# A recurrent attention and two feed-forward layers: decay products stored head first, and feed-forward units that follow the weight blocks as they are made

## The chip, the cores and the metric

The kernel runs on one core of a Trainium2 chip. The metric is the device time of one execution in microseconds (us). Three executions of the kernel before took 1311.25, 1311.51 and 1312.43 us; the median is 1311.51 us. One more execution was profiled.

## The reference

Three parts follow each other. The first is a recurrence over 768 time steps for 4 batches x 8 heads = 32 heads of width 40, each with a 40 x 40 state. The other two are gated feed-forward layers over 3072 rows of 320 values.

```python
for t in range(S):
    y[:, :, t] = np.einsum('bhd,bhde->bhe', rt, state)
    Sa = np.einsum('bhde,bhe->bhd', state, at)
    state_decay = state * wt[:, :, None, :] - np.einsum('bhd,bhe->bhde', Sa, bt)
    state = state_decay + np.einsum('bhd,bhe->bhde', vt, kt)
...
g = x @ w_gate                            # 320 x 1536
silu = g * (1.0 / (1.0 + np.exp(-g)))     # layer 1; layer 2 has only the sigmoid here
x = (silu * (x @ w_val)) @ w_out          # 1536 x 320
```

## The kernel before

**The recurrence by chunks.** Time is cut into 12 chunks of 64 steps (`C = 64`). Inside a chunk everything is matrix products; between chunks only the state is carried. The keys, `a` and the results of a chunk are scaled by running products of the decay `w` along the chunk (powers `p`) and by their inverses (`r`). For chunks 0 to 3 these products come from scans on VectorE. For chunks 4 to 11 GpSimd multiplies them up ahead of time, four chunks at once, with one head and chunk on each partition (`powers`, lines 228 to 269), and SyncE stores them to DRAM: `pd[m]` and `rd[m]`, at line 268. There are two such groups, so 8 stores of `p` and 8 of `r`. Both groups use the same two tiles (`wp`, `wq`), so the second group may write them only when the stores of the first have landed. The loads of a later chunk read them back with time on the partitions: `load_p` (`pn`, line 350, read twice for each chunk), `loads` (`ip`, line 338) and `ends` (line 372).

**What a chunk consists of.** `prep_a(m)` scales and builds `kps` products, `prep_b(m)` inverts a triangular matrix (on VectorE, with two trips through DRAM for chunks from 3 on: `xd`, lines 534 and 536), `chain(m)` carries the state and `post(m)` makes the output rows. `merge` (line 913) interleaves the generators of these parts by a table of steps and offsets (`NA`, `NB`, ... lines 924 to 939): while `chain` and `post` of chunk m run, `prep_b` of m + 1 and `prep_a` of m + 2 are emitted beside them, and `ahead(m)`, which is the first feed-forward layer on the output of chunk m - 1. A scheduler then sets the order on each engine; every engine carries out its own instructions in that order.

**The feed-forward layers by units.** The 3072 rows are 12 blocks of 256 rows, one for each chunk. The 1536 columns are 12 weight blocks. A unit is one block of rows with one weight block: `gate` makes 16 matrix products of 128x256 (line 1105) and the gating (lines 1109 to 1112), `add` sums 6 products of 128x320 into two accumulators (line 1121). Every weight arrives as 64-bit floats and is split into a high and a low part by `load_w`, in three thirds; the last step of the last third is line 1031 on GpSimd. A layer has 12 x 12 = 144 units, the two together 288.

**Which units run when.** During the recurrence memory has room for few weight blocks of layer 1 (`w1`): three early, two more during chunk 1, and seven that `more` (line 1312) puts into tiles that the recurrence gives up near its end. `extra(m)` runs block m with the blocks that exist when it starts: `used.append(len(w1))` (line 1332). After the recurrence `stream` runs what is left of layer 1 for each row block (`w1[used[blk]:]`, adding to the part already in DRAM), while the weights of layer 2 are converted (`ahead`, line 1361), and then layer 2.

**Names in the rows.** `tp` transposes, `kps`, `zps`, `xps`, `qps`, `ups`, `sps`, `aps`, `yps` are matrix products of the recurrence, `am` is the masked `aps`, `gv` is the gate product during the recurrence and `g` after it, `hh` and `hl` are the high and low part of a unit's gated values, `po` the accumulators. `part_...` are several small tiles of the recurrence that share memory; the tile `an`, which line 386 writes, and the one that line 534 reads are both such pieces of one `part`. `raw` is a third of a weight block as it arrives, `dt` and `ds` its work tiles.

## Time and profile before

| | before |
|---|---|
| median of three executions | 1311.51 us |
| the profiled execution, its own time | 1313.94 us |
| span of its instructions | 1312.2 us |
| PE busy in the span | 1212.9 us (92%) |
| DVE, ACT, POOL busy | 714.0, 600.9, 562.0 us |

PE is TensorE's matrix products, PEld its weight loads, DVE VectorE, ACT ScalarE, POOL GpSimd, SP SyncE, which here only issues DMAs. PEclk is the TensorE clock that was granted, 1.0 being full. Between stretches of the program the limits differ: the recurrence with the units beside it ends about 677 us into the span; what follows are feed-forward units alone. In a row of an engine's timeline the square bracket is the idle time of the engine before the instruction, and what ended it.

### The profile page before, as it was taken

The page shows a single profiled execution, that of the slowest core. Times are in us where ns is not written, and L with a number is a line of the kernel's source. Part 1 is how long each engine was busy: PE and PEld are TensorE (multiplying, and loading weights), DVE is VectorE, ACT ScalarE, POOL GpSimd, SP SyncE. Part 2 cuts the span into 40 slices and gives each one's busy share as a digit, 9 for nine tenths or more (in the row PEclk, how much of TensorE's full clock was granted, in tenths as well). Part 3 has the DMA queues.
Part 4 walks back from the last instruction along what each step waited for, and adds up shares of the span by engine and source line. Part 5 has one row for each costly group of instructions (what it writes and reads, how often), then busy time and mean ns, then how long its engine had stood idle before and what let it go on. Part 6 is the DMA issues. An engine that isn't in the chain of part 4 may idle for free.

```text
span 1312.2 us, 34352 instructions
## 1 busy us (share of the span) xinstructions
PE 1212.9 (92%) x14209; PEld 1164.6 (89%) x14209; DVE 714.0 (54%) x1434; ACT 600.9 (46%) x1447; POOL 562.0 (43%) x749
## 2 busy tenths in 40 slices
PE   5487889999999999898899999999999999999996
PEld 4477778989988998797889999999999999999996
DVE  6858668886668867757789877222111212212121
ACT  8464655655665566254434444223333333333331
POOL 5757352232233233457778988322222222222221
PEclk7666977999999999799899999999999999999998
DMA  7554844433454344343455542221000000000000
GB/s 214 118 135 120 201 120 123 127 105 113 131 150 126 89 117 108 104 108 112 169 175 171 185 159 94 95 97 45 11 23 23 23 23 23 23 23 23 11 11 14
DMA packets 153061, 126.12 MB, mean 96 GB/s; under 512 B 100928, under 2 KB 131136, under 8 KB 152640
## 3 DMA queue, kind: packets, MB, share of 16 engines
q1 hardware_dynamic: 152896, 123.84, 32.7%
q8 instruction: 113, 1.85, 0.6%
q14 instruction: 52, 0.43, 0.1%
HBM read 92.05 MB, written 31.76 MB: 94 GB/s over the span
## 4 chain that ended last, share of the span: by engine, by line
PE 58%; DVE 20%; ACT 8%; DMA 4%; issue 4%; POOL 3%; SPq 1%; ACTq 0%; POOLq 0%; DVEq 0%
PE g L1105 31%; PE po L1121 16%; DVE pr L521 4%; PE gv L1105 3%; DVE part L527 3%; PE kps L481 2%; DMA wt<-in_a_w_dram 2%; PE tp L366 1%; PE aps L854 1%; DVE dt L1008 1%; DVE am L863 1%; ACT bn L490 1%; DVE lq L493 1%; ACT bn L491 1%; DVE g L1110 1%
## 5 line engine op out<-in xcount | busy, mean ns | idle before, releaser
L1105 PE MATMUL g<-x,w 128*128 128x256 f32 x3520 | 485.9, 282 | 2.1 <-DVE g L1110 1.3
L1105 PEld LDWEIGHTS g<-x,w 128*128 128x128 f32 x3520 | 456.7, 189 | 3.2 <-DVE g L1110 2.1
L1112 POOL TENSOR_TENSOR hl<-g,hh 128x256 fp32r<-128x256 f32 x288 | 225.8, 785 | 474.1 <-ACT hh L1111 466.3
L1110 DVE TENSOR_TENSOR g<-g,g 128x256 f32<-128x256 f32 x220 | 92.9, 423 | 361.8 <-PE g L1105 353.3
L1121 PE MATMUL po<-w,hh 128*128 128x320 f32 x1152 | 228.9, 312 | 4.8 <-ACT hh L1111 4.7
L1111 ACT CAST hh<-g 128x256 fp32r<-128x256 f32 x288 | 116.7, 406 | 252.9 <-DVE g L1110 222.8
L1121 PEld LDWEIGHTS po<-w,hh 128*128 128x128 f32 x1152 | 177.1, 189 | 6.6 <-ACT hh L1111 6.1
L1105 PE MATMUL gv<-x,w 128*128 128x256 f32 x1088 | 160.7, 298 | 7.9 <-DVE g L1110 6.0
L1105 PEld LDWEIGHTS gv<-x,w 128*128 128x128 f32 x1088 | 143.4, 199 | 12.9 <-DVE g L1110 9.2
L1121 PE MATMUL po<-w,hl 128*128 128x320 f32 x576 | 143.7, 314 | 2.5 <-POOL hl L1112 2.5
L1109 ACT ACTIVATE g<-g 128x256 f32<-128x256 f32 x220 | 84.3, 384 | 130.4 <-PE g L1105 123.9
L1025 POOL TENSOR_TENSOR dt<-dt,w 128x384 f32<-128x384 f32 (+1 forms) x72 | 80.4, 1118 | 82.3 <-DVE ds L1012 36.8
L1121 PEld LDWEIGHTS po<-w,hl 128*128 128x128 f32 x576 | 93.7, 190 | 3.8 <-POOL hl L1112 3.5
L493 DVE TENSOR_TENSOR lq<-kps,part 64x256 f32<-64x256 f32 x96 | 40.5, 421 | 84.2 <-ACT bn L491 66.4
L521 DVE TENSOR_TENSOR pr<-part,sn 128x4 f32<-128x4 f32 (+4 forms) x135 | 74.7, 553 | 3.6
L481 PE MATMUL kps<-lq,kbt 104*128 104x128 f32 x384 | 62.6, 314 | 8.4 <-DVE lq L493 6.9
L527 DVE TENSOR_REDUCE part<-pr 128x2 f32<-128x4 f32 (+4 forms) x135 | 66.5, 493 | 2.8
L1023 ACT CAST w<-dt 128x384 fp32r<-128x384 f32 (+1 forms) x72 | 35.5, 495 | 66.9 <-DVE dt L1008 62.2
L481 PEld LDWEIGHTS kps<-lq,kbt 104*128 104x128 f32 x384 | 54.8, 220 | 12.4 <-issue 4.2
L854 PE MATMUL aps<-rbd,ut 104*128 104x128 f32 x384 | 56.3, 292 | 5.5 <-DVE am L863 5.1
L1007 DVE TENSOR_SCALAR dt<-dt 128x384 int32<-128x384 int32 (+1 forms) x72 | 44.9, 624 | 30.0 <-POOL dt L1004 29.6
L490 ACT ACTIVATE bn<-kps 32x256 f32<-32x256 f32 x96 | 35.8, 373 | 50.0 <-PE kps L481 43.9
(182 smaller groups left out, 1670.9 us busy)
## 6 DMA issues: line engine op xcount, KB each, us to landing
raw<-in_w_dram SPq DMA_DIRECT2D x48, 384.0 KB
xd<-x SPq DMA_DIRECT2D x12, 896.0 KB
x<-xd SPq DMA_DIRECT2D x12, 896.0 KB
raw<-in_w_dram SPq DMA_DIRECT2D x24, 320.0 KB
ld<-in_a_kb_dram SPq DMA_DIRECT2D x22, 320.0 KB
ld<-rd SPq DMA_DIRECT2D x32, 160.0 KB
pn<-pd SPq DMA_DIRECT2D x32, 160.0 KB
ld<-in_a_a_dram SPq DMA_DIRECT2D x12, 320.0 KB
```

What stands on the lines that cost most here:

```text
L481: nc.tensor.matmul(kps[:, n].rearrange("p h t -> p (h t)"), lhsT=kbt[0:PW, n, :], rhs=lq[m % 3][0:PW, 4 * g4 + n].rearrange("p h t -> p (h ...
L493: nc.vector.tensor_tensor(out=lq[m % 3][o, q, h2, :], in0=kps[o, :, h2, :], in1=mask[o, None, :].to_broadcast([64, 4, C]), op=ALU.mult,)
L521: nc.vector.tensor_tensor(out=o, in0=xs[:, 0:kk, None, 0:n].to_broadcast([P, kk, 2, n]), in1=sn[:, None, n : n + 2, 0:n].to_broadcast([P, ...
L527: nc.vector.tensor_reduce(out=xs[:, 0:kk, n : n + 2], in_=o, axis=AX.X, op=ALU.add)
L854: nc.tensor.matmul(aps[:, n, h2], lhsT=ut[0:PW, x, 2 * h2 : 2 * h2 + 2].rearrange("p u s -> p (u s)"), rhs=rbd[0:PW, x, h2].rearrange("p b ...
L1025: sub(out=tf, in0=tf, in1=w.bitcast(F32), op=ALU.subtract)
L1105: nc.tensor.matmul(gv[n], lhsT=p, rhs=q, start=e == 0, stop=e == len(seq) - 1)
L1109: nc.scalar.activation(out=g, in_=gv[0], func=AF.Silu if silu else AF.Sigmoid)
L1110: nc.vector.tensor_tensor(out=g, in0=gv[1], in1=g, op=ALU.mult)
L1111: nc.scalar.copy(out=hh, in_=g)
L1112: self.heng.tensor_tensor(out=hl, in0=g, in1=hh.bitcast(F32), op=ALU.subtract)
L1121: self.nc.tensor.matmul(ops[u], lhsT=p[:, us], rhs=q, start=first and n == 0, stop=last and n == 2)
```

## The change

**Storage.** `pd[m]` and `rd[m]` are laid out head first, `[heads, time, 40]`, as the tiles are, so a store takes 65 x 40 or 64 x 40 values of one head in one run (10,400 or 10,240 bytes) instead of 160 bytes at a time. The loads of chunks 4 to 11 gather: `pn` takes 16 heads x 64 steps in pieces of 40 values (160 bytes; before 2,560), `ip` 8 heads x 64 steps (160 bytes; before 1,280) in two DMAs where there was one.

**Units.** `ffn` asks for the next weight block after each unit, so a block that was appended to `w1` meanwhile is used too; the number used is noted at the end. The numbers by row block change from 3, 5 (eight times), 6, 8, 11, in all 68, to 3, 5 (eight times), 7, 10, 12, in all 72. Row block 11 is then finished, and the stream after the recurrence has 11 jobs of layer 1, with 72 units instead of 76. The two tiles for a block's rows alternate by place in that list.

```diff
--- before.py
+++ after.py
@@ -264,8 +264,8 @@
             rows = slice(32 * j, 32 * j + 32)
             for i, x in enumerate((p[rows], q[rows, 1:])):
                 to = (pd, rd)[i]
-                to[m] = dr.tile([C + 1 - i, H * B, D], F32, tag=f"{'pr'[i]}d{m}", name="pr"[i] + "d", bufs=1)
-                nc.sync.dma_start(out=to[m].rearrange("t h d -> h t d"), in_=x)
+                to[m] = dr.tile([H * B, C + 1 - i, D], F32, tag=f"{'pr'[i]}d{m}", name="pr"[i] + "d", bufs=1)
+                nc.sync.dma_start(out=to[m], in_=x)
             yield
 
     def all_powers():
@@ -335,10 +335,11 @@
             dma(out=x, in_=kb[m, bp])
 
             for u in range(2):
-                dma(
-                    out=ip[HALF[u]].rearrange("t (c x) -> t c x", c=2),
-                    in_=rd[m].rearrange("t (c u x) d -> t c u (x d)", c=2, u=2)[:, :, bp],
-                )
+                for c in range(2):
+                    dma(
+                        out=ip[HALF[u]].rearrange("t (c x d) -> t c x d", c=2, d=D)[:, c],
+                        in_=rd[m].rearrange("(c u x) t d -> t c u x d", c=2, u=2)[:, c, bp],
+                    )
             yield x, ip
 
     def load_p(m):
@@ -347,7 +348,10 @@
             nc.sync.dma_start(out=pn, in_=pq[m])
             return pn
         for b2 in range(2):
-            nc.sync.dma_start(out=pn[HALF[b2]], in_=pd[m][0:C, 16 * b2 : 16 * b2 + 16].rearrange("t h d -> t (h d)"))
+            nc.sync.dma_start(
+                out=pn[HALF[b2]].rearrange("t (h d) -> t h d", d=D),
+                in_=pd[m][16 * b2 : 16 * b2 + 16, 0:C].rearrange("h t d -> t h d"),
+            )
         return pn
 
     def loads_late(m):
@@ -369,7 +373,7 @@
         return ps
 
     def ends(m):
-        nc.sync.dma_start(out=pairs(pe[0:NS])[:, 0], in_=pd[m][C].rearrange("(s h) d -> s h d", h=2))
+        nc.sync.dma_start(out=pairs(pe[0:NS])[:, 0], in_=pd[m][:, C].rearrange("(s h) d -> s h d", h=2))
         yield
         ps = ptp.tile([P, 4, P], F32, tag="tp", name="pep")
         nc.tensor.transpose(ps[0:PW, 0, 0:NS], pe[0:NS, 0], ident[0:NS, 0:NS])
@@ -1125,14 +1129,16 @@
     def ffn(self, x, ws, silu, tag):
 
         ops, pend = self.sums(tag), None
-        for f, w in enumerate(ws):
-            h = self.gate(x, w, silu)
+        self.o, f = ops, 0
+        while f < len(ws):
+            h = self.gate(x, ws[f], silu)
             if pend is not None:
-                self.add(ops, *pend)
-            pend = w, h, f == 0, f == len(ws) - 1
-            yield
-        self.add(ops, *pend)
-        self.o = ops
+                self.add(ops, *pend, False)
+            pend = ws[f], h, f == 0
+            f += 1
+            yield
+        self.add(ops, *pend, True)
+        self.used = f
 
     def stream(self, jobs):
 
@@ -1329,11 +1335,11 @@
                 if m == 0:
                     ffn.raw = raws
                 if m >= 0:
-                    used.append(len(w1))
                     x = ffn.split(ys.pop(m))
                     nc.sync.dma_start(out=xd[m], in_=x.bitcast(F32))
                     yield
-                    yield from ffn.ffn(x, w1[: used[m]], True, "po")
+                    yield from ffn.ffn(x, w1, True, "po")
+                    used.append(ffn.used)
                     for u in range(2):
                         ob = h_p.tile([P, DM], F32, tag="ob", name="ob", bufs=1)
                         nc.scalar.copy(out=ob, in_=ffn.o[u])
@@ -1360,8 +1366,10 @@
 
             ahead = load_w2()
 
+            left = [blk for blk in range(NB) if used[blk] < NF]
+
             def load_x(blk):
-                ffn.x = (x_q, x_p)[blk % 2]
+                ffn.x = (x_q, x_p)[left.index(blk) % 2]
                 x = ffn.new_x()
                 nc.sync.dma_start(out=x.bitcast(F32), in_=xd[blk])
                 yield x
@@ -1372,7 +1380,7 @@
                 nc.sync.dma_start(out=xin[:, :, 0:DM], in_=src)
                 nc.sync.dma_start(out=xin[:, :, DM:], in_=src[:, :, 256:DM])
                 yield
-                ffn.x = (x_q, x_p)[blk % 2]
+                ffn.x = (x_q, x_p)[(len(left) + blk) % 2]
                 yield from ffn.split_steps([xin[:, 0], xin[:, 1]])
 
             parts = {}
@@ -1383,7 +1391,7 @@
                     nc.sync.dma_start(out=part, in_=xs[1][2 * blk : 2 * blk + 2].rearrange("u p e -> p u e"))
                 if 1 <= f <= 3:
                     next(ahead, None)
-                if blk == NB - 1 and f == NF - 1 - used[blk]:
+                if blk == left[-1] and f == NF - 1 - used[blk]:
                     for _ in ahead:
                         pass
 
@@ -1428,7 +1436,7 @@
                 flag.append(fl)
 
             flag, jobs, seen = [], [], []
-            for blk in range(NB):
+            for blk in left:
                 jobs.append((w1[used[blk] :], True, "po", load_x(blk), partial(each1, blk), partial(end1, blk)))
             for blk in range(NB):
                 jobs.append((w2, False, "po", split_x(blk), partial(check, blk), partial(end2, blk)))
```

The change makes the scheduler set another order in places. On POOL, just after the first group's powers, `L261` is the second group's first write to `wp`. Before:

```order
L1004 TENSOR_SCALAR dt<-dt 128x384
L238 TENSOR_TENSOR wq<-wq 128x320 x2
L1025 TENSOR_TENSOR dt<-dt,w_1450 128x384
L238 TENSOR_TENSOR wq<-wq 128x320
L1027 TENSOR_TENSOR w_1450<-dt,ds 128x256
L1029 TENSOR_TENSOR w_1450<-dt,ds 64x128
L238 TENSOR_TENSOR wq<-wq 128x320
L261 MEMSET wp 128x40
L238 TENSOR_TENSOR wq<-wq 128x320
L1004 TENSOR_SCALAR dt<-dt 128x384
L238 TENSOR_TENSOR wq<-wq 128x320 x2
```

And now:

```order
L1008 TENSOR_SCALAR dt<-dt 128x384
L238 TENSOR_TENSOR wq<-wq 128x320 x2
L261 MEMSET wp 128x40
L1029 TENSOR_TENSOR dt<-dt,w_1450 128x384
L238 TENSOR_TENSOR wq<-wq 128x320
L1031 TENSOR_TENSOR w_1450<-dt,ds 128x256
L1033 TENSOR_TENSOR w_1450<-dt,ds 64x128
L238 TENSOR_TENSOR wq<-wq 128x320 x2
L1008 TENSOR_SCALAR dt<-dt 128x384
L238 TENSOR_TENSOR wq<-wq 128x320 x2
L1029 TENSOR_TENSOR dt<-dt,w_1450 128x384
```

The write to `wp` stands five rows earlier, right behind the second of the `wq` products and before the conversion of a weight third; nothing else moves there.

On DVE, in the same part of the program, `L241` clamps the second group's decays, once for `wp` and once for `wq`; `sps` and `kps` are products of chunks 0 and 1. Before:

```order
L726 TENSOR_TENSOR part_86<-sps,part_86 40x4x2x40 x2
L1008 SCALAR_TENSOR_TENSOR dt<-raw,dt 128x384
L726 TENSOR_TENSOR part_86<-sps,part_86 40x4x2x40 x2
L727 TENSOR_TENSOR part_86<-part_86,pend 104x4x2x40
L1012 TENSOR_SCALAR ds<-dt 128x384
L241 TENSOR_SCALAR wp<-wq 128x2560
L727 TENSOR_TENSOR part_86<-part_86,pend 104x4x2x40
L493 TENSOR_TENSOR lq_210<-kps,part_86 64x4x64
L1013 SCALAR_TENSOR_TENSOR ds<-raw,ds 128x384
L863 TENSOR_TENSOR am<-aps,part_86 128x512
L241 TENSOR_SCALAR wq<-wq 128x2560
```

And now:

```order
L497 TENSOR_TENSOR lq_210<-kps,part_86 64x4x64
L241 TENSOR_SCALAR wp<-wq 128x2560
L497 TENSOR_TENSOR lq_210<-kps,part_86 64x4x64
L1011 TENSOR_SCALAR dt<-dt 128x384
L241 TENSOR_SCALAR wq<-wq 128x2560
L1012 SCALAR_TENSOR_TENSOR dt<-raw,dt 128x384
L730 TENSOR_TENSOR part_86<-sps,part_86 40x4x2x40 x2
L497 TENSOR_TENSOR lq_210<-kps,part_86 64x4x64
L730 TENSOR_TENSOR part_86<-sps,part_86 40x4x2x40 x2
L1016 TENSOR_SCALAR ds<-dt 128x384
L731 TENSOR_TENSOR part_86<-part_86,pend 104x4x2x40
```

Both clamps now stand ahead of the additions of `sps` (L730, before L726), where they stood behind them.

On SP, in one chunk of the middle stage, from the loads of `pn` on. Before:

```order
L350 DMA pn<-pd 64x640 x2
L335 DMA ld<-in_a_kb_dram 128x640
L338 DMA ld<-rd 64x2x320 x2
L1334 DMA xd<-x 128x1792
L534 DMA xd<-part_88 1024x1x32 x2
L356 DMA part_197<-in_a_v_dram 64x640 x2
L536 DMA part_212<-xd 32x16x32 x4
L335 DMA ld<-in_a_kb_dram 128x640
```

And now:

```order
L351 DMA pn<-pd 64x16x40 x2
L335 DMA ld<-in_a_kb_dram 128x640
L339 DMA ld<-rd 64x8x40 x4
L1339 DMA xd<-x 128x1792
L538 DMA xd<-part_88 1024x1x32 x2
L360 DMA part_197<-in_a_v_dram 64x640 x2
L540 DMA part_212<-xd 32x16x32 x4
L335 DMA ld<-in_a_kb_dram 128x640
```

Four gathering loads of `rd` stand in front of the stores `xd<-part` where there were two, and one more pair behind; in every second chunk only one stands in front. On PE and POOL the order inside these chunks is the same as before, but for two `po` products.

On PE, at the end of the recurrence, while the last chunk's `aps` and `yps` are made; `w_8423` before and `w_8485` now are the eighth weight block. Before:

```order
L854 MATMUL aps<-rbd,ut 128x128 x4
L1105 MATMUL gv<-x,w_8423 128x256 x8
L1051 MATMUL xtp<-ident,ysb 128x128 x3
L1121 MATMUL po_8518<-w_7801,hh 128x320 x2
L1121 MATMUL po_8519<-w_7801,hh 128x320 x2
L854 MATMUL aps<-rbd,ut 128x128 x4
L1121 MATMUL po_8518<-w_7801,hl 128x320
L1121 MATMUL po_8519<-w_7801,hl 128x320
L1121 MATMUL po_8518<-w_8423,hh 128x320 x2
L1121 MATMUL po_8519<-w_8423,hh 128x320 x2
L885 MATMUL yps<-part_197,rbd 64x40 x16
```

And now:

```order
L858 MATMUL aps<-rbd,ut 128x128 x4
L1109 MATMUL gv<-x,w_8527 128x256 x3
L1109 MATMUL gv<-x,w_8745 128x256 x2
L1125 MATMUL po_8580<-w_8485,hh 128x320 x2
L1125 MATMUL po_8581<-w_8485,hh 128x320 x2
L1109 MATMUL gv<-x,w_8745 128x256 x9
L1125 MATMUL po_8580<-w_8485,hl 128x320
L1125 MATMUL po_8581<-w_8485,hl 128x320
L1109 MATMUL gv<-x,w_8745 128x256 x5
L1055 MATMUL xtp<-ident,ysb 128x128 x3
L889 MATMUL yps<-part_197,rbd 64x40 x16
L889 MATMUL yps<-tkb_91,am 64x40 x16
```

Where only the last two units' `po` products were left to run between the last `aps` and `yps`, the products of a ninth and a tenth weight block now stand there (`w_8527`, `w_8745`).

## Rows read from the trace of the kernel before

**Rows 1.** Busy time by stretch: us, PE, PEld, DVE, ACT, POOL, PEclk, DMA share, GB/s.

```profile
54.00:97.00 43.00, 32.62 (x672) 28.91 (x672) 25.84 (x45) 23.81 (x54) 24.64 (x31) 0.62 0.65 144
212.00:503.00 291.00, 282.43 (x4652) 263.14 (x4652) 220.99 (x448) 179.22 (x436) 84.32 (x98) 1.00 0.44 119
503.00:546.00 43.00, 36.88 (x566) 34.21 (x565) 32.84 (x71) 20.66 (x49) 15.71 (x20) 0.88 0.30 85
546.00:588.00 42.00, 39.23 (x637) 37.03 (x637) 25.39 (x52) 21.42 (x49) 23.91 (x33) 0.92 0.43 120
588.00:641.00 53.00, 43.56 (x552) 40.28 (x550) 38.60 (x63) 22.95 (x57) 38.24 (x52) 0.94 0.32 101
641.00:677.00 36.00, 33.08 (x238) 31.71 (x238) 28.79 (x63) 15.54 (x41) 27.37 (x35) 0.94 0.62 202
677.00:1312.00 635.00, 621.97 (x4919) 620.24 (x4919) 215.38 (x431) 222.21 (x563) 257.37 (x354) 0.99 0.19 60
```

**Rows 2.** Page, costliest groups: count, then busy us and mean ns.

```profile
L1105 PE MATMUL g<-x,w 128*128 128x256 f32 x3520 | 485.9, 282 | 2.1 <-DVE g L1110 1.3
```

**Rows 3.** SP's queue in order of time: start us, us, what it issues.

```profile
54.51 7.90 SPq L268 DMA_DIRECT2D pd<-wp  x4
...
70.27 7.22 SPq L268 DMA_DIRECT2D rd<-wq  x4
77.60 2.63 SPq L993 DMA_DIRECT2D raw<-in_w_dram  x2
81.96 0.33 SPq L236 DMA_DIRECT2D wq<-in_a_w_dram  x1
...
136.72 7.71 SPq L268 DMA_DIRECT2D rd<-wq  x4
```

**Rows 4.** POOL in order of time, 60 to 75 us.

```profile
67.05 0.14 POOL L261 MEMSET wp<- 128x40 f32 x1 [2.52 <-DMA pd<-wp]
```

**Rows 5.** DVE in order of time, 60 to 95 us.

```profile
68.52 1.01 DVE L1007 TENSOR_SCALAR dt<-dt 128x384 int32<-128x384 int32 x1 [5.48 <-POOL dt L1004]
...
83.75 0.43 DVE L493 TENSOR_TENSOR lq<-kps,part 64x256 f32<-64x256 f32 x1 [5.52 <-ACT bn L491]
...
88.96 1.49 DVE L241 TENSOR_SCALAR wp<-wq 128x2560 f32<-128x2560 f32 x1
```

**Rows 6.** ACT in order of time, 78 to 90 us.

```profile
82.63 0.55 ACT L1001 ACTIVATE dt<-raw 128x384 f32<-128x384 f32 x1 [1.05 <-DMA raw<-in_w_dram]
```

**Rows 7.** Short stretches, SP alone: us, PEclk, DMA share, GB/s.

```profile
55.00:63.00 8.00, 0.50 1.01 171
85.00:90.00 5.00, 0.97 0.57 208
562.00:565.00 3.00, 1.00 0.59 92
```

**Rows 8.** SP's queue inside one chunk of the middle stage.

```profile
332.67 1.62 SPq L350 DMA_DIRECT2D pn<-pd  x2
...
335.59 1.30 SPq L534 DMA_DIRECT2D xd<-part  x2
```

**Rows 9.** POOL in the same chunk.

```profile
341.41 1.55 POOL L386 TENSOR_TENSOR part<-ld,pn 128x640 f32<-128x640 f32 x1 [4.24 <-DMA xd<-part]
344.32 0.74 POOL L1112 TENSOR_TENSOR hl<-g,hh 128x256 fp32r<-128x256 f32 x1 [1.36 <-ACT hh L1111]
```

**Rows 10.** PE in the same chunk.

```profile
346.26 0.31 PE L1121 MATMUL po<-w,hl 128*128 128x320 f32 x1
```

**Rows 11.** PE while the last chunk is finished, 588 to 641 us.

```profile
600.98 0.85 PE L1121 MATMUL po<-w,hh 128*128 128x320 f32 x4 [1.46 <-ACT hh L1111]
...
636.99 1.13 PE L885 MATMUL yps<-part,rbd 104*64 104x40 f32 x32 [2.90 <-DVE am L863]
```

**Rows 12.** POOL, last step of two weight blocks.

```profile
612.10 0.87 POOL L1031 TENSOR_TENSOR w<-dt,ds 128x320 fp32r<-128x320 f32 x1
...
642.93 0.86 POOL L1031 TENSOR_TENSOR w<-dt,ds 128x320 fp32r<-128x320 f32 x1
```

## The prediction

> **What bounds the kernel now.** I read busy time by stretch first. From 677 us to the end PE is busy 621.97 of 635.00 us at a granted clock of 0.99 [rows 1]: feed-forward units alone, bound by PE. From 212 to 503 us it is busy 282.43 of 291.00 us at full clock [rows 1], so that stage too is almost only PE's own work. The reader is to see that what is left lies elsewhere: before 212 us, as from 54 to 97 us, where PE is busy 32.62 of 43 us and the clock is 0.62, and between 503 and 677 us, where the recurrence runs out [rows 1]. Next come the timelines, to see who is waited for there. In the early stretch SP stands at its stores of the powers: four stores hold its queue 7.90, 7.22 and 7.71 us (three of the four groups of four) [rows 3], POOL waits 2.52 us for them to land [rows 4], DVE 5.48 us for POOL [rows 5], and ACT 1.05 us for a weight third that was issued behind them [rows 6]. While the last chunk is finished, PE waits for the units' `hh` and for `am`, 1.46 and 2.90 us [rows 11]. In the middle stage POOL waits 4.24 us for the stores `xd<-part` [rows 9], but PE hardly waits.
>
> So an edit pays here only if it shortens the early stretch or puts PE's work into the holes between 546 and 677 us; and it costs if it opens holes between 212 and 503 us.
>
> **Stores (part one of the change).** All 16 stores carry 5.28 MB. From 55 to 63 us nothing but such 160-byte pieces moved: 171 GB/s at a DMA share of 1.01. From 85 to 90 us the decays came in runs of 10,240 bytes: 208 GB/s at 0.57, that is 365 GB/s for a full share [rows 7]. A store of 0.333 MB thus goes from 1.95 to 0.91 us, and four in a row from some 7.5 us to 3.6 us. SP's freed time is not itself on the path; what stood behind it is.
>
> - POOL's early write to `wp` waits for the first four stores. They will have landed at about 54.5 + 3.6 = 58 us, before POOL gets there: 2.52 us [rows 4]. The same 2.52 us leave DVE's wait for POOL [rows 5]; that is the same gain, counted once.
> - The `rd` stores start about 2.5 us earlier and hold SP to about 71 us instead of 77.5, so the weight thirds are issued from there and ACT's wait goes: 1.05 us [rows 3, 6].
> - The second group's decays can be loaded at about 72 us instead of 81.96 [rows 3]; 1.31 MB at 365 GB/s are 3.6 us, so they are there near 77 us. The two clamps of 1.49 us [rows 5] now stand early in DVE's queue, and DVE has a hole of 5.52 us that ends at 83.75 [rows 5]. They go into it and leave the dense stretch after 88.96: 2.98 us. If the load is late, all of DVE's queue stands behind the clamp, the additions of `sps` first; that is why I don't take more than their own length.
>
> Sum 6.6 us. Against it: PE ran at half clock, 0.50 in the row from 55 to 63 us [rows 7], and was busy for most of the stretch, so part of what DVE and POOL gain waits for PE. The second pair of store groups I count at nothing, because PE has other work by then. The least is nothing, or a loss the size of one new stall like DVE's (5.5 us), since PE's and DVE's order changes in this whole stretch; the most is all of SP's freed time, 4 x (7.5 - 3.6) = 15.5 us. I take a gain of 5 us, near the named waits.
>
> **Loads (part one).** A chunk's loads of `pn` and `rd` carry 1.31 MB, in 12 DMAs instead of 8. No row has 160-byte pieces loaded. The nearest is 562 to 565 us, almost only the loads `part<-xd` in pieces of 128 bytes: 92 GB/s at a share of 0.59, or 156 GB/s [rows 7], against 365. So 8.4 us instead of at least 3.6: 4.8 us more of the DMA engines for each chunk, which takes the share from 0.44 [rows 1] to about 0.56 over some 41.6 us. That alone is hidden.
>
> What is late next is `xd<-part`, for it stands behind these loads on SP, and POOL waits for it. Half of the extra bytes lie in front, 2.4 us, and two more issues; two issues take 1.30 us where each makes 1,024 pieces and 1.62 us for the coarser `pn` [rows 8], so the count of pieces doesn't matter and I take 0.65 each, 1.3 us. `xd<-part` lands up to 3.7 us later. Behind POOL's waiting instruction stands the unit's `hl`, which had 1.36 us of idle before it and was done 1.20 us before PE took it up (344.32 + 0.74 against 346.26) [rows 9, 10]. Slack 2.56 us, so PE waits at most 1.1 us. In every second chunk only one `rd` load stands in front and the slack suffices. Eight chunks: 0 to 4.5 us. A gain is excluded, since every load only gets longer. I take a loss of 1.5 us.
>
> Here the Trainium skill (DMA: Bandwidth & Descriptors, section Specifications) speaks against the change: it wants transfers of at least 512 bytes for line rate and says that below this the engine reads, modifies and writes. The trace agrees in the rate: 156 to 169 GB/s for the small pieces against 365 [rows 7]. If the rule asks no more than that, the sum stays as it is.
>
> **Units (part two).** After 677 us 3520 products are 220 units of 16 [rows 2], so one costs 635 / 220 = 2.89 us. Four fewer there: 11.5 us off the end. The four come back earlier: one in 546 to 588 us, two in 588 to 641, one in 641 to 677. PE's idle time in these is 2.8, 9.4 and 2.9 us [rows 1]. What they fill is the gain. Near the end of the second stretch the new order puts the products of two more weight blocks exactly where PE waited 2.90 us for `am` [rows 11]; the waits near 601 us lie earlier than the added units and stay. I take 4 us filled there, 1 us in the first stretch, nothing in the last, which is units alone already. The clock in these stretches is 0.92 to 0.94 [rows 1]; 6% of 43.56 us are 2.6 us, and I give 1 us of it back for the closed hole. Gain 5 + 1 = 6 us. The ends: all 11.5 us, or nothing, and below nothing by some 2 us if the added `hl` (0.74 us each, rows 9) and its gating stand in front of the recurrence on POOL, ACT and DVE.
>
> The weight blocks are there: the tenth is done at 613 us and used near 636, the twelfth at 643.8 and used near 675 [rows 12]. Costing nothing: the job that goes (its loads and stores lie at a DMA share of 0.19 [rows 1]), the alternation of the two row tiles, the stop flag. Layer 2's weight conversion loses some 11 us of room; DVE is busy 215 of 635 us there [rows 1].
>
> **Sum.** -5 + 1.5 - 6 = -9.5 us. The profiled execution took 1313.9 us, so 1304.4 by its own measure; it was 2.4 us above the median of 1311.5, which gives 1302.0 for a median.
>
> **Rivals.**
>
> 1. The small pieces into on-chip memory cost twice what the nearest row says (78 GB/s), and the middle stage pays. Then half a chunk's loads takes 8.4 us in front of `xd<-part` instead of 1.8, which with the issues is 7.9 us later; less the slack, PE waits 5.3 us in four chunks, and about 0.8 us in the four with one `rd` load in front: 24 us. With the gains 1311.5 - 11 + 24 = 1324.5, slower. It decides from about 4 us of delay of `xd<-part` in every chunk. For it: no row shows such loads, and POOL does wait there [rows 9]. Against it: 128-byte loads and 160-byte stores ran alike [rows 7]. A second cost for a partial write, beside the rate, would be the skill's rule above at its worst; no run here shows it yet. Chance 0.12.
> 2. The added units fill nothing, because PE's holes come from the recurrence's own chain and only shift: 1311.5 - 5 + 1.5 = 1308. For it: the larger holes are waits for ACT and DVE [rows 11], which the units load too. Chance 0.12.
> 3. The early gain is missing: PE at half clock is the bound there [rows 7], and the stores never were. 1311.5 + 1.5 - 6 = 1307. Chance 0.13.
> 4. All of SP's freed time was on the path: 1311.5 - 15.5 + 1.5 - 6 = 1291.5. Against it: the second pair lies beside busy PE. Chance 0.10.
>
> **How the numbers follow.** The forecast has 0.53, with its own range from 1296 to 1308. Two tenths of a per cent, 2.6 us, is about what a measurement tells from no change. Faster than 1308.9: 0.50 of the forecast, 0.07 of rival 2, 0.11 of rival 3 and all of rival 4, together 0.78. Within: 0.10. Slower: rival 1 with 0.12. The range for 8 in 10 goes from 1291 to 1314: it takes in the forecast, rivals 2 and 3, part of 4 and a stall in the early stretch, and leaves rival 1 out.
>
> **What would show it.** Stores: SP's groups at line 268 below 4 us, no POOL wait at line 261, the clamps before 84 us, and the first units' stage ending some 5 us earlier. Loads: the period of the middle stage, 41.6 us, longer by less than 0.5 us; if POOL's wait for `xd<-part` grows by 4 us or more and PE waits for `hl`, rival 1 is right. Units: 72 `gv` units, the stream begins at about 677 - 3.5 + 5.5 = 679 us or a little later, 216 units of 2.89 us behind it, and no wait for `am` near the last `yps`. The forecast fails if the stream begins after 685 us.

## The result and the profile after

The changed kernel takes 1302.21 us (median of five runs, 1298.81 to 1303.58), the kernel before 1312.43 us beside it: a ratio of 0.9913, 95% interval 0.9901 to 0.9925. The profiled execution took 1302.28 us, its span is 1300.6 us. The total came out as forecast (1302.0), but by another sum, so that it agrees is luck. The stretches of [rows 1], read again in the changed kernel (the last one ends with its span):

```profile
54.00:97.00 43.00, 32.74 (x683) 28.91 (x676) 25.71 (x42) 22.67 (x52) 27.48 (x34) 0.67 0.49 143
212.00:503.00 291.00, 279.13 (x4584) 260.81 (x4584) 224.27 (x452) 176.08 (x430) 85.59 (x98) 1.00 0.51 118
503.00:546.00 43.00, 37.82 (x665) 35.14 (x666) 33.88 (x73) 24.46 (x60) 16.71 (x22) 1.00 0.39 102
546.00:588.00 42.00, 39.72 (x667) 37.17 (x663) 27.38 (x55) 21.43 (x51) 22.79 (x33) 1.00 0.47 126
588.00:641.00 53.00, 47.76 (x594) 45.35 (x591) 40.59 (x69) 26.77 (x66) 43.45 (x57) 1.00 0.33 105
641.00:677.00 36.00, 32.41 (x249) 31.56 (x248) 30.83 (x68) 15.34 (x39) 25.81 (x36) 0.99 0.72 234
677.00:1300.00 623.00, 610.22 (x4822) 608.96 (x4821) 208.95 (x418) 217.65 (x552) 253.93 (x349) 0.99 0.18 56
```

What changed most is the granted clock from 503 to 641 us: 0.88, 0.92 and 0.94 before, 1.00 now. To place the time, both traces are divided at the same instructions: the first `qps` product of each chunk's joint chain (the `chain` of chunks 3 to 11, which carries all heads at once), the last `yps` product, and the first `g` product of the stream. These are single profiled executions; the one before was 1.5 us above the median beside it.

| us | chunk 9 begins | chunk 9 | chunk 10 | chunk 11, to its last `yps` | tail to the stream | stream |
|---|---|---|---|---|---|---|
| before | 499.8 | 46.9 | 41.3 | 51.2 | 37.6 | 635.3 |
| after | 503.3 | 41.9 | 41.9 | 46.3 | 41.8 | 625.4 |
| difference | +3.5 | -5.0 | +0.6 | -4.9 | +4.2 | -9.9 |

So the recurrence is 3.5 us late up to chunk 9, then 5 us faster in chunk 9 and again in chunk 11, though more units run beside it (7 and 10 `gv` units instead of 6 and 8 in chunks 10 and 11). The tail holds 12 units instead of 11, and the stream 216 instead of 220:

```profile
L1109 PE MATMUL g<-x,w 128*128 128x256 f32 x3456 | 478.6, 282 | 3.3 <-DVE g L1114 2.6
```

**The early stretch.** The stores became as short as the arithmetic said, in SP's queue of the changed kernel (start, time, what is issued):

```profile
53.85 3.74 SPq L268 DMA_DIRECT2D pd<-wp  x4
...
68.46 3.34 SPq L268 DMA_DIRECT2D rd<-wq  x4
...
77.94 0.35 SPq L236 DMA_DIRECT2D wq<-in_a_w_dram  x1
...
132.13 4.29 SPq L268 DMA_DIRECT2D rd<-wq  x4
```

These answer to [rows 3]: 7.90, 7.22 and 7.71 us became 3.74, 3.34 and 4.29. ACT's wait for `raw` [rows 6] is gone. But POOL still waits at line 261, now 5.6 us earlier: the first four stores had landed only at 61.4 us, 3.8 us after SP had issued the last of them, and the write that waits for them had moved up. And DVE waits 7.11 us for the decays at a clamp that stands early in its queue, with `sps`'s additions behind it (85.65 us before, 89.41 now). POOL:

```profile
61.41 0.14 POOL L261 MEMSET wp<- 128x40 f32 x1 [2.56 <-DMA pd<-wp]
```

DVE:

```profile
83.52 1.50 DVE L241 TENSOR_SCALAR wp<-wq 128x2560 f32<-128x2560 f32 x1 [7.11 <-DMA wq<-in_a_w_dram]
...
86.09 2.15 DVE L241 TENSOR_SCALAR wq<-wq 128x2560 f32<-128x2560 f32 x1
...
89.41 0.99 DVE L730 TENSOR_TENSOR part<-sps,part 40x320 f32<-40x320 f32 x2
```

The first unit's `gv` nevertheless begins at 127.5 us instead of 131.4. That is an effect of the order on PE and no gain of the recurrence: these products now stand ahead of a group of `kps` products that they followed before, and that group begins later than before. Before:

```profile
130.28 1.13 PE L481 MATMUL kps<-lq,kbt 104*128 104x128 f32 x8 [0.45 <-DVE lq L493]
...
131.39 0.71 PE L1105 MATMUL gv<-x,w 128*128 128x256 f32 x4
```

After:

```profile
127.45 1.20 PE L1109 MATMUL gv<-x,w 128*128 128x256 f32 x4
...
130.78 2.08 PE L485 MATMUL kps<-lq,kbt 104*128 104x128 f32 x8
```

From 127 to 145 us PE is then busy nearly all the time, at half clock. Before:

```profile
127.00:145.00 18.00, 15.97 (x368) 14.23 (x368) 12.63 (x31) 12.32 (x28) 10.04 (x14) 0.83 0.81 132
```

After:

```profile
127.00:145.00 18.00, 17.32 (x233) 15.55 (x221) 9.39 (x25) 10.11 (x23) 5.48 (x7) 0.53 0.59 170
```

PE is busy 1.35 us more, with fewer products done (233 against 368, of mixed sizes). By the start of chunk 3's chain the changed kernel is 2.8 us late (252.3 against 249.5).

**The loads.** The periods of chunks 4 to 8 are 41.35 to 41.64 us, before 41.68 to 41.70. Only chunk 3's grew, 41.86 to 43.43 us: there PE waits 2.22 us for a unit's `hl`, which stands on POOL behind the wait for `xd<-part` (9.34 us instead of 7.11).

```profile
268.36 0.56 PE L1125 MATMUL po<-w,hl 128*128 128x320 f32 x2 [2.22 <-POOL hl L1116]
```

**Chunk 9, which the forecast does not mention.** DVE around the last unit there, before:

```profile
531.96 0.61 DVE L899 TENSOR_TENSOR ysb<-yps,pn 128x320 f32<-128x320 f32 x2
532.49 0.55 DVE L1008 SCALAR_TENSOR_TENSOR dt<-raw,dt 128x384 int32<-128x384 int32 x1
...
533.37 0.35 DVE L1012 TENSOR_SCALAR ds<-dt 128x384 int32<-128x384 int32 x1
...
534.03 0.55 DVE L1013 SCALAR_TENSOR_TENSOR ds<-raw,ds 128x384 f32<-128x384 uint32 x1
...
535.59 0.41 DVE L1110 TENSOR_TENSOR g<-gv,g 128x256 f32<-128x256 f32 x1
...
537.97 0.68 DVE L863 TENSOR_TENSOR am<-aps,part 128x512 f32<-128x512 f32 x1
```

After:

```profile
535.09 0.61 DVE L903 TENSOR_TENSOR ysb<-yps,pn 128x320 f32<-128x320 f32 x2
...
537.00 0.42 DVE L1114 TENSOR_TENSOR g<-gv,g 128x256 f32<-128x256 f32 x1
...
538.43 0.68 DVE L867 TENSOR_TENSOR am<-aps,part 128x512 f32<-128x512 f32 x1
```

The three weight steps (L1008, L1012, L1013) are no longer between `ysb` and `g`: 3.6 us from one to the other became 1.9. Before, PE waited there for `hh`:

```profile
536.49 1.44 PE L1121 MATMUL po<-w,hh 128*128 128x320 f32 x4 [2.54 <-ACT hh L1111]
```

And behind the wait the clock fell. Before, 10 us from 535, then after, 8 us from 537, where PE has no such wait:

```profile
535.00:545.00 10.00, 7.47 (x78) 6.78 (x78) 9.15 (x14) 1.26 (x3) 0.73 (x1) 0.54 0.33 102
```

```profile
537.00:545.00 8.00, 5.61 (x91) 4.94 (x90) 7.83 (x15) 1.77 (x4) 1.85 (x3) 1.00 0.27 83
```

### The profile page after: what moved, and what is told of

It reads as the page before. It is cut to its first block, busy times and chain, and to the rows that moved or that the text cites. A ratio compares the mean times of both kernels' runs of the same rounds, so it can differ in the third digit from the quotient of the medians.

```text
span 1300.6 us, 34364 instructions
## 1 busy us (share of the span) xinstructions
PE 1204.2 (93%) x14209; PEld 1158.9 (89%) x14209; DVE 710.7 (55%) x1432; ACT 600.4 (46%) x1447; POOL 561.7 (43%) x749
## 4 chain that ended last, share of the span: by engine, by line
PE 59%; DVE 19%; ACT 8%; issue 5%; DMA 4%; POOL 3%; SPq 0%; POOLq 0%; ACTq 0%; DVEq 0%
PE g L1109 32%; PE po L1125 16%; DVE pr L525 4%; PE gv L1109 2%; DVE part L531 2%; PE kps L485 2%; PE aps L858 1%; PE tp L370 1%; DVE lq L497 1%; DMA wt<-in_a_w_dram 1%; ACT bn L495 1%; DVE g L1114 1%; DVE am L867 1%; DVE part L822 1%; ACT bn L494 1%
## 5 line engine op out<-in xcount | busy, mean ns | idle before, releaser
L1109 PE MATMUL g<-x,w 128*128 128x256 f32 x3456 | 478.6, 282 | 3.3 <-DVE g L1114 2.6
L1109 PEld LDWEIGHTS g<-x,w 128*128 128x128 f32 x3456 | 449.7, 190 | 4.0 <-DVE g L1114 3.1
L1109 PE MATMUL gv<-x,w 128*128 128x256 f32 x1152 | 167.8, 294 | 5.3 <-DVE g L1114 3.2
L1109 PEld LDWEIGHTS gv<-x,w 128*128 128x128 f32 x1152 | 149.9, 195 | 8.5 <-DVE g L1114 4.4
L1029 POOL TENSOR_TENSOR dt<-dt,w 128x384 f32<-128x384 f32 (+1 forms) x72 | 79.0, 1098 | 72.8 <-ACT w L1027 39.2
L485 PE MATMUL kps<-lq,kbt 104*128 104x128 f32 x384 | 62.4, 312 | 11.5 <-DVE lq L497 8.6
L1011 DVE TENSOR_SCALAR dt<-dt 128x384 int32<-128x384 int32 (+1 forms) x72 | 48.7, 677 | 30.5 <-POOL dt L1008 30.3
L370 PE MATMUL tp<-ident,part 128*104 128x128 f32 x288 | 46.0, 297 | 15.3 <-ACT pend L178 6.3
```

Of the source, the lines that this page charges most:

```text
L370: t = nc.tensor.transpose(ps[0 : x.shape[1], n, :], x, ident)
L485: nc.tensor.matmul(kps[:, n].rearrange("p h t -> p (h t)"), lhsT=kbt[0:PW, n, :], rhs=lq[m % 3][0:PW, 4 * g4 + n].rearrange("p h t -> p (h ...
L1029: sub(out=tf, in0=tf, in1=w.bitcast(F32), op=ALU.subtract)
L1109: nc.tensor.matmul(gv[n], lhsT=p, rhs=q, start=e == 0, stop=e == len(seq) - 1)
```

## The experiments

My first theory (A) was that the units part gives the 10 us and the storage part only closes the hole of chunk 9, a gain that its early loss takes back. When that fell, the second (A2) was that the new order on DVE, which the storage part sets off, gives them; its rival B2 was the stores and loads themselves. "Order" below is the order of instructions on each engine. The table has the times between the marks in us; the ratio is to the kernel before in the same comparison, where its median was 1312.4 to 1314.0. The first six rows have the order of before on PE, DVE, ACT and POOL up to chunk 9 ("old order" below), the others that of the storage part ("new order"):

| | first `gv` | chunk 3 | 9 | 10 | 11 | tail | stream | median | ratio |
|---|---|---|---|---|---|---|---|---|---|
| before | 131.4 | 41.9 | 46.9 | 41.3 | 51.2 | 37.6 | 635.3 | 1312.4 | |
| e2_units | 132.2 | 41.6 | 46.9 | 42.8 | 50.1 | 44.9 | 626.7 | 1311.8 | 0.9982 [0.9967, 0.9997] |
| e3b_second4 | 132.1 | 41.6 | 46.9 | 43.7 | 49.7 | 47.5 | 626.6 | 1312.1 | 0.9982 [0.9969, 0.9994] |
| f1_edge | 133.7 | 42.1 | 47.0 | 41.2 | 43.9 | 38.0 | 636.2 | 1306.5 | 0.9947 [0.9930, 0.9964] |
| f1_first | 131.7 | 42.0 | 50.2 | 39.9 | 47.6 | 39.6 | 637.6 | 1314.4 | 1.0006 [0.9994, 1.0018] |
| f3_units_edge | 133.4 | 41.7 | 46.8 | 42.5 | 51.7 | 40.9 | 624.5 | 1308.3 | 0.9965 [0.9951, 0.9980] |
| e1_storage | 127.9 | 44.8 | 42.3 | 39.9 | 44.0 | 39.2 | 636.2 | 1303.8 | 0.9924 [0.9906, 0.9942] |
| f2_undo | 127.4 | 44.9 | 44.2 | 40.8 | 43.9 | 39.5 | 636.4 | 1308.5 | 0.9955 [0.9937, 0.9972] |
| after | 127.5 | 43.4 | 41.9 | 41.9 | 46.3 | 41.8 | 625.4 | 1302.2 | 0.9913 [0.9901, 0.9925] |
| e3_first4 | 127.3 | 45.1 | 42.3 | 42.2 | 46.1 | 41.9 | 625.7 | 1300.8 | 0.9894 [0.9875, 0.9913] |
| f4_checks_late | 127.8 | 45.2 | 42.3 | 42.4 | 46.7 | 37.8 | 623.2 | 1296.0 | 0.9870 [0.9850, 0.9891] |
| f5_storage_checks_late | 127.2 | 45.0 | 42.2 | 40.1 | 43.3 | 33.5 | 635.1 | 1297.6 | 0.9883 [0.9867, 0.9900] |
| f6_edge31 | 126.0 | 45.1 | 42.3 | 42.0 | 44.8 | 39.1 | 622.4 | 1293.7 | 0.9856 [0.9839, 0.9872] |
| f7_p5 | 127.2 | 45.0 | 42.3 | 42.1 | 45.1 | 39.1 | 622.2 | 1294.1 | 0.9856 [0.9833, 0.9880] |

**e1_storage and e2_units: one part each.** The edits are the diff's pieces up to `ends`, and those from `ffn` on.

> The storage part alone: head-first layout for chunks 4 to 11, units as before. Theory A (the end moves by the units, and by a hole of the recurrence that the storage's new order closes): early stage about 3 to 4 us later by the start of chunk 4's joint chain, middle stage unchanged, the 47 us period from 500 us back to about 42, the stream 635 us as before: 1310 us, -1.5 to -2.5 against before. Theory B (that hole is closed by the units' order, not by the storage): the period stays at 47 us and only the early loss is left, 1315.5 us, slower by 3. If my predicted terms were right (early gain 5, loads 1.5), 1309 us with an early mark 5 us sooner, not later.

> The units part alone: layout, stores and loads as before. Theory A: all four units are filled in beside the recurrence, the stream loses 4 x 2.9 = 11.5 us less what the stage before it grows; the early marks are those of before, the period from 500 us stays at 47 us: 1302 us, -10 against before. Theory B: the period from 500 us shrinks to 42 here too: 1297 us. My predicted term alone: 1306.5.

Theory A fell: the storage part alone gives a ratio of 0.9924, some 10 us, and the units part alone 0.9982, some 2.4 us (0.4 to 4.3). In the storage part's trace chunks 9 to 11 are 4.6, 1.4 and 7.2 us shorter. In the units part's trace the stream loses 8.6 us, but chunk 10 and the tail grow by 1.5 and 7.3; the period of chunk 9 stays at 46.9, as A had it.

**e3_first4 and e3b_second4: the new layout for half of the chunks.** Both parts, with the loads to match; `n == 2` in the second, shortened at the dots:

```diff
-                to[m] = dr.tile([H * B, C + 1 - i, D], ...)
-                nc.sync.dma_start(out=to[m], in_=x)
+                if n == 1:
+                    to[m] = dr.tile([H * B, C + 1 - i, D], ...)
+                    nc.sync.dma_start(out=to[m], in_=x)
+                else:
+                    to[m] = dr.tile([C + 1 - i, H * B, D], ...)
+                    nc.sync.dma_start(out=to[m].rearrange("t h d -> h t d"), in_=x)
```

> Both parts, but head first only for chunks 4 to 7; chunks 8 to 11 are stored and loaded as before. The order on PE, DVE, ACT and POOL is that of the changed kernel row by row, only SP's differs. Theory A: what the early stage loses comes with that order and not with the stores' time, and the scattered loads of chunks 8 to 11 cost nothing: within 1.5 us of the changed kernel's 1302, the 42 us period from 500 us too. Rival C (the loads of 160-byte pieces cost something that the order hides): 2 us faster than the changed kernel in the periods of chunks 8 to 11. Rival D (SP's time at the second group's stores near 120 to 140 us is on the path): 3 to 4 us slower than the changed kernel, in the marks before 250 us.

> Both parts, but head first only for chunks 8 to 11; chunks 4 to 7 are stored and loaded as before. The order on PE, DVE, ACT and POOL is that of the kernel with the units part alone, row by row. Theory A: within 1.5 us of the units part alone, about 1302; no early loss. Rival C: about 2 us slower than it, in the periods of chunks 8 to 11. Rival D: 3 to 4 us faster than it, in the marks before 250 us (stores 3.7 us instead of 7.4, twice).

With the same order come nearly the same times, whatever the layout of chunks 8 to 11: e3_first4 beside after, e3b_second4 beside e2_units. Chunks 9 to 11 agree within 0.9 us in each pair, the periods of chunks 4 to 8 within 0.13 us in the first and 0.03 in the second; the second pair's tails are 2.6 us apart, and the first pair's periods of chunk 3 are 1.7 apart. So C falls. Of D the second pair's trace shows something (2.6 us sooner at 249 us), but the first pair's shows the opposite (e3_first4 is there 3.5 us sooner, not later), and the second pair's medians agree (1312.1 and 1311.8). What matters goes with the layout of the first group, and so with the order. For chunk 9 that leaves little else than the order: in e3_first4 the chunks that are loaded from then on lie as before, and chunk 9 still takes 42.3 us.

**f1_edge and f1_first: the order without the layout.** Storage and units of before; one weight third (number 18) gets its place on DVE prescribed, by a dependency that only sets the order of two instructions of that engine (shortened, with its two numbers put in).

```diff
+            dt = ts(out=t, in0=t, scalar1=5, scalar2=2, ...)
+            if self.one_bank and self.n - 1 == 18:
+                self.tc.add_manual_dep(dt.ins, self.ams[39].ins.name, ...)  # f1_first: self.gs[42]
```

> Before's storage and units, and one more order on DVE: the steps of one weight third (the one that stood between ysb and the unit's g product of the ninth chunk) may not come before that chunk's last am. By this DVE's order in the last chunk becomes that of the storage part alone, row by row; storage itself is untouched. Theory A2 (the 10 us of the storage part are the order of the weight steps against the recurrence's own steps on DVE in the last three chunks; the storage only set it off): period from 500 us 47 to 43 us, the last chunk from its joint chain to its last yps 51 to 44 or 45 us, 1302 to 1304 us. Rival B2 (the 10 us come from the stores or loads themselves): 1313 us like before.

> The same with the third ordered only behind the unit's g product of that chunk, so its steps come between g and the two am. DVE's order in the last chunk stays close to before's (ten weight steps between the joint chain's start and its sps additions, not ten with g ahead of them). Theory A2: the period from 500 us 47 to 44, the last chunk 51 us as before: 1309 to 1310 us. Rival B2: 1313 us.

f1_edge settles it for chunk 11: 51.2 became 43.9 us, as in the storage part alone (44.0), and the median is 7.2 us lower (1306.5), with not a byte stored or loaded otherwise. DVE in chunk 11 before (its chain begins at 588.1):

```profile
594.63 0.33 DVE L1007 TENSOR_SCALAR dt<-dt 128x320 int32<-128x320 int32 x1 [2.83 <-POOL dt L1004]
...
600.07 0.42 DVE L1110 TENSOR_TENSOR g<-gv,g 128x256 f32<-128x256 f32 x1
...
609.46 0.92 DVE L1013 SCALAR_TENSOR_TENSOR ds<-raw,ds 128x320 f32<-128x320 uint32 x1
610.30 2.01 DVE L818 TENSOR_TENSOR part<-sps,part 40x320 f32<-40x320 f32 x4
```

And in f1_edge (its chain begins at 586.6):

```profile
594.32 0.42 DVE L1122 TENSOR_TENSOR g<-gv,g 128x256 f32<-128x256 f32 x1 [3.49 <-ACT g L1121]
595.55 0.62 DVE L1012 TENSOR_SCALAR dt<-dt 128x320 int32<-128x320 int32 x1 [0.81 <-POOL dt L1009]
...
603.41 1.39 DVE L1020 SCALAR_TENSOR_TENSOR dt<-raw,dt 128x384 int32<-128x384 int32 x1
604.73 2.01 DVE L818 TENSOR_TENSOR part<-sps,part 40x320 f32<-40x320 f32 x4
```

The first unit's `g` stands ahead of eight weight steps instead of behind them, 7.7 instead of 12.0 us after the chain's start, and the state's additions follow at 18.1 instead of 22.2. The wait of 1.46 us for `hh` [rows 11] goes, and PE waits 1.11 instead of 2.90 us for `am`. For chunk 9 the expectation was wrong, and so the 1302 to 1304 us were missed: the weight steps left, but six steps of the inversion (`pr`, `part`) came ahead of `g`, and PE waited 2.86 us in place of 2.54, in f1_edge:

```profile
535.43 1.43 PE L1133 MATMUL po<-w,hh 128*128 128x320 f32 x4 [2.86 <-ACT hh L1123]
```

f1_first has the same wait of 2.86 us, and its chunk 9 grew to 50.2 us where 44 was expected; chunk 11 went to 47.6 where 51 was expected. In sum there is no gain: 1314.4 us, nearer to what B2 said (1313) than to A2's 1309 to 1310. For chunk 9 these two runs do not bear A2 out.

**f2_undo: the storage part with the third ordered behind `ysb`.**

```diff
+                self.tc.add_manual_dep(dt.ins, self.ysbs[36].ins.name, ...)   # third 18
```

> The storage part alone, with that weight third ordered behind the first ysb of the ninth chunk, so that two of its steps stand between ysb and the g product again, and the tenth chunk has before's order; the last chunk keeps the order of the storage part. Theory A2: of the storage part's 10 us, 1 to 4 go again in the period from 500 us (42 back to 44 to 46), the last chunk stays at 44: 1305 to 1307 us. Rival B2: 1303.8 as the storage part alone.

Chunks 9 and 10 lost 1.9 and 0.9 us, chunk 11 kept its 43.9. The median, 1308.5 us, is 4.7 us above the storage part alone (single runs 1304.0 to 1310.2) and a little above the range of A2; from chunk 9 on the marks account for 3.2 us. Before chunk 9 its profile is 2.9 us later, which is no more than profiles of one order differ by. So of the 4.6 us that chunk 9 gains in the storage part, this order takes 1.9 back; no run shows the rest by moving the order alone.

**f3_units_edge: f1_edge's order with the units part.**

> The units part alone with the order of f1_edge (third behind the ninth chunk's last am); in the last chunk the order on DVE lies between that of the units part alone and that of both parts. Theory A2: the period from 500 us 47 to 43, the last chunk 1 to 3 us shorter than in the units part alone: 1305 to 1308 us. Rival B2: 1311.8 as the units part alone.

The time, 1308.3 us, is at the upper end of the range, but not for the reasons given: chunks 9 and 11 did not shorten, the tail did (44.9 to 40.9). The profiled execution was the fastest of 12, 4.2 us under their median, so its marks do not give the median's gain.

**f4, f5, f6: the same idea at the next place.** In the changed kernel PE waits 2.14 us for the last `gv` unit's `g` before the stream. PE:

```profile
675.20 4.45 PE L1109 MATMUL g<-x,w 128*128 128x256 f32 x24 [2.14 <-DVE g L1114]
```

DVE's rows show who stands ahead:

```profile
672.41 0.49 DVE L1421 TENSOR_REDUCE wacc<-wt 128x1 f32<-128x320 f32 x1 [0.93 <-DMA wt<-in_a_w_dram]
672.81 0.47 DVE L1422 TENSOR_REDUCE wacc<-wt 128x1 f32<-128x320 f32 x1
...
674.35 0.47 DVE L1422 TENSOR_REDUCE wacc<-wt 128x1 f32<-128x320 f32 x1
674.74 0.41 DVE L1114 TENSOR_TENSOR g<-gv,g 128x256 f32<-128x256 f32 x1
```

The reductions (L1421, L1422) check the decays and are written beside layer 2's units; the scheduler had moved them up. f4 ties them to those units, f6 also puts one more weight third behind chunk 11's first `ysb`.

```diff
+                            tc.add_manual_dep(red.ins, ffn.gated.ins.name, ...)
+LATE = {31: 45}   # f6 only: third 31 behind ysb 45
```

> The changed kernel with one more order on DVE: the 48 reductions that check the decays (0.47 us each, between 651 and 697 us in the changed kernel, beside the weight steps) may not come before the layer 2 unit that they are written behind. The weight steps' order in the last three chunks is that of the changed kernel. Theory A2 (at the end of the recurrence PE waits for what stands ahead on DVE): the wait of 2.14 us for g at 675 us and the half clock behind it go, the first units of the stream come at 2.9 instead of 3.2 us: 1297 to 1299 us, -3 to -5 against the changed kernel. Rival (PE is the bound from 640 us on and the waits only move): 1302 us.

> The storage part alone with the same 48 reductions moved: units as before, so 76 units of layer 1 stand in the stream. Theory A2: 3 to 4 us less than the storage part alone (1303.8): 1300 to 1301 us. Rival: 1303.8. Beside f4 it prices the units part once more: A2 says 2 to 3 us between the two.

> f4_checks_late with the four steps of one more weight third on DVE put behind the last chunk's first ysb instead of ahead of it (PE waited 1.20 us for that ysb at 622.8 us). Theory A2: the wait goes and the last chunk is about 1 us shorter than in f4: 1296 to 1298 us. Rival (the third's weight block is then late for its unit and the wait moves there): as f4 or 1 us slower.

All three went A2's way, and each is faster than its range: the tail is 4.0 us shorter in f4, 5.7 in f5, and the stream 2.2 and 1.1; chunk 11 is 1.9 us shorter in f6 than in f4. f4's median is 6 us under the changed kernel's, f6's another 2.4, though their intervals overlap. f6 beats both kernels: 1293.7 us, 0.9856 of before. Between f5 and f4 the units part is worth 1.6 us by the medians, with overlapping intervals; 2 to 3 were expected.

**f7_p5: f6 with chunk 5's `p` time first.** The diff is e3's with `m == 5` and `pd` alone.

> f6_edge31 with the p products of the sixth chunk (number 5) alone stored time first and loaded in pieces of 2,560 bytes, as before; the order on PE, DVE and ACT is that of f6_edge31 row by row. In the period of chunk 3 (45.1 us in f6_edge31, 41.9 before) these loads stand in front of xd<-part, and PE waits some 2.2 us for a unit's hl behind it. Theory L (the small pieces delay xd<-part there beyond its slack): 0.33 MB at 365 instead of 156 GB/s are 1.2 us less in front, so the wait falls to about 1 us and the period to 43.5 to 44 us; the others stay at 41.4 to 41.7. Rival (the wait comes from the new order alone): the period stays at 45. Time 1292 to 1294 us either way.

The period stayed at 45.0 and PE's wait at 2.24 us. Theory L falls for the `p` pieces. Whether the `rd` pieces or the order cause that wait was not told apart, since `rd` of chunk 5 in the old layout changes the order.

## Why the prediction was right and wrong

- **Stores, -5 us: wrong, no gain at chunk 3.** The step that failed is that a gain at the named waits reaches the end. In the eight kernels with the new order a first group of `kps` begins at 124.3 us on average, in the six with the old one at 125.7: the recurrence is 1.4 us ahead there, not 5. The next group begins at 130.7 and 130.8, and the start of chunk 2's chain at 163.2 against 162.3, chunk 3's at 249.1 against 248.0, where single profiles of one order spread over 5.4 us (new) and 3.5 (old). The first `gv` does come 5 us sooner (127.3 against 132.4), but only because it moved ahead of that next group. The granted clock from 127 to 145 us is 0.53 to 0.70 in the eight of the new order, 0.76 to 0.83 in the six of the old. So rival 3 came true in what it says of the gain; that PE's half clock is the reason no run shows. One named wait, POOL's 2.52 us, did not even go: the stores were taken to have landed when SP has issued them (58 us), and they landed at 61.4. The load of the decays was taken to start near 72 us; it started at 77.94, and the stall behind the clamp that the forecast named came true. Its rate of 171 GB/s for 160-byte pieces comes from a row in which pieces of 3,072 bytes (weight thirds) carry a quarter of the bytes, so not those pieces alone moved there; a 160-byte piece took 16 ns, with 16 engines 160 GB/s, which would change little in the sum.
- **Loads, +1.5 us: the size was off, and the place.** Chunk 3's period is 44.8 us in the new order and 41.8 in the old: +3.0, with the sign and the chain that the step named (POOL's wait for `xd<-part`, then `hl`), but in one period, not spread over eight. Whether the loads or the order make it is open (f7_p5). The small pieces of chunks 8 to 11, loaded in the periods of chunks 6 to 9, change these by at most 0.05 us (e3b_second4 beside e2_units). Rival 1 falls: its 24 us are nowhere.
- **Units, -6 us: too large, 2.4 us.** Two sizes failed. The stream lost 8.6 us in the units part alone, not 11.5: at its start a unit does not take 2.89 us (the first four took 8.4 us together before, and 10.4 in the units part alone). And before the stream 6.5 us are added (7.3 in the tail and 1.5 in chunk 10, less 1.1 before chunk 9 and 1.1 in chunk 11), where 5.5 were expected. The tail is where one added unit was to cost its 2.89 us. For this term rival 2 (nothing gained) is the nearer one. In the new order the 72 units are there as forecast, and the stream begins at 675.2 instead of 679 us.
- **What was missing: some -11.6 us** (13.2 in chunks 9 to 11 of e1_storage, of which the tail takes 1.6 back). The forecast showed on two pieces of the new order what moves in the early stretch, and did not look at DVE's order in chunks 9 to 11, where it read the waits of [rows 11] as the recurrence's own and took those near 601 us to stay. They came from weight steps that stood in front of `g`, the additions and `am`: f1_edge shows it for chunk 11, by the order alone; for chunk 9 it rests on the rows, on e3_first4 and, for 1.9 us, on f2_undo. The total agreed by luck, because this took the place of gains of the stores and units that did not come.

## What to carry to other kernels

Where a scheduler sets the order, an edit in one stage can move instructions in every later one: compare the order at each wait of the profile, not only beside the edit, and price what stands in front of the instruction that is waited for. Then prescribe the order that proved good (one dependency gave 7 us, the 48 of f4 another 6), instead of leaving it to an edit elsewhere, and look at what comes in front in its place (f1_first gained nothing). To follow a gain through a reordered stretch, take several marks: an instruction may come sooner only because it was moved, as the first `gv` was here.

## What the runs showed of the hardware

Here a wait of PE cost more than its length. With the 2.54 us at 536 us before, the granted clock was 0.54 over the ten microseconds from 535 (mostly the lower of the two levels, 1.2 GHz), and chunk 9 was 4.6 to 5.0 us longer than in the new order (f2_undo aside); in the changed kernel, where PE waits no more than 1.57 us there, it stayed at 1.00.

Some of DVE's weight steps stretch when GpSimd works beside them. The step `ds<-raw,ds` (128x384) takes 0.56 us alone; in the kernel before, in front of the `am` that PE waits 2.90 us for [rows 11], it took 2.75:

```profile
633.59 2.75 DVE L1013 SCALAR_TENSOR_TENSOR ds<-raw,ds 128x384 f32<-128x384 uint32 x1
636.26 0.68 DVE L863 TENSOR_TENSOR am<-aps,part 128x512 f32<-128x512 f32 x1
```

POOL meanwhile:

```profile
633.30 0.57 POOL L1029 TENSOR_TENSOR w<-dt,ds 64x128 fp32r<-64x128 f32 x1
633.84 0.98 POOL L1025 TENSOR_TENSOR dt<-dt,w 128x384 f32<-128x384 f32 x1
634.79 0.71 POOL L1112 TENSOR_TENSOR hl<-g,hh 128x256 fp32r<-128x256 f32 x1
635.48 0.44 POOL L1004 TENSOR_SCALAR dt<-dt 128x320 f32<-128x320 f32 x1
```

The Trainium skill (SBUF — State Buffer, section Terms) says that VectorE and GpSimd share one pair of ports, which one instruction holds to its end while the other is blocked. The trace agrees as far as it goes: the step begins inside the first of four POOL instructions in a row and ends 0.42 us after the last of them. The one other such step of that kernel beside four of them took 2.79 us.

The small pieces were no surprise: the 160-byte loads took 15.6 ns each on average in the changed kernel, the 160-byte stores of before 16 ns. Of the read, modify and write that the Trainium skill (DMA: Bandwidth & Descriptors, section Specifications) names below 512 bytes, no run here shows a cost beside the lower rate.
